# Masks of the first batch from 64-row tiles of TensorE, and block means of v from 32-column tiles

## The chip, the cores and the metric

One core of one Trainium2 chip runs the kernel; the other cores are idle. The metric is the device time of one execution in microseconds (us), from runs on the chip. A profiled execution also has a span: the time from its first to its last instruction.

## The reference, cut to what matters

Attention over 4 batches, 8 heads, 768 positions and 64 channels, in which a query sees the keys fewer than 16 positions away and, beside them, 24 block summaries (the maximum of each 32 keys, with the mean of the 32 values). Its output goes through a max-out layer.

```python
k_sum = k.reshape(B, H, nb, 32, D).max(axis=3)
v_sum = v.reshape(B, H, nb, 32, D).mean(axis=3)
mask_l = np.abs(pos[:, None] - pos[None, :]) < 16
scores_s = scale * einsum('bhsd,bhnd->bhsn', q, k_sum) + np.log(32)
scores_l = np.where(mask_l, scale * q @ k.T, -1e9)
a = softmax(concatenate([scores_l, scores_s]))
x = a @ concatenate([v, v_sum])        # to (3072 tokens, 512)
out = np.maximum(x @ w1, x @ w2) @ w_out
```

## The kernel before, in words

The max-out is rewritten: max(x w1, x w2) w_out is x (w1 w_out) + relu(x (w2 - w1)) w_out. So the kernel prepares wd = w2 - w1 (VectorE, line 662) and w1o = w1 w_out (TensorE, line 679), and each piece of 256 tokens needs "hidden" (x times wd, line 695, then a relu), and "out" (x times w1o, line 726, and the relu times w_out, line 733).

Attention is cut into batch, pair of heads (hp 0 to 3), and group (grp 0 to 2) of 256 queries. For each hp, "prep" casts k and q to bf16, turns them (on TensorE, line 471, or with a DMA transpose, line 475) and builds kx: for each of 12 tiles of 64 queries, 128 columns of keys, among them the 24 block maxima. "Scores" (line 540) multiplies 64 channels of one head with the tile's kx as the stationary operand and 64 queries as the moving one. The two heads of a pair (a = 0, 1) lie in partitions 0 to 63 and 64 to 127, so their products are matmuls on 64 of the 128 rows of the array, and they write two different PSUM banks. Then come exp on ScalarE over two pairs at once (line 558), "values" (line 594, the weights of a tile as stationary operand of 64 columns), a reciprocal (line 613), a product (line 616, "x"), and the turn of x (line 631 on TensorE in batch 0, line 622 by DMA transpose later).

The mask. `hide` holds 0 where a key is seen and -2^60 where not, as [128 keys, 64 queries] for an even and an odd tile (indices 0 and 1), and for the last two tiles (2 and 3, where 3 differs from 1). Batches 1 to 3 multiply the weights by a 0/1 mask on VectorE (line 566). Batch 0 adds `hide` on TensorE ahead of the scores: in each half task (one pair, one group; 12 of them) two matmuls (a = 0, 1), the identity stationary on all 128 rows, `hide` moving with 256 columns (line 531). TensorE thereby goes from 128-row to 64-row matmuls and back in each half task; the code calls this mode "NS" (N: whole array, S: 64 rows, V: column tiles).

The means of v. v is cast into vx with 32 positions in each 128-row chunk left over for a block mean. For batch 0 the means are kept apart (line 415, "apart"). For batches 1 to 3 `later_sums` adds up blocks with `amean`, whose columns mark the blocks: 6 chunks times two halves (u) of the head pairs, 12 matmuls on 64-column tiles with 256 moving columns (line 432). One copy ("means", 128x256) brings the sums into the staging tile `stg`, and four copies ("all sums", 32 partitions x 1584) put them into vx for both halves of the tile pairs w. On POOL only two of the four may run.

The order. Nothing is scheduled at run time. `Plan` gives each call of `op` a number in order of creation; ORDER lists the numbers in the order in which they are issued, HOMES gives each its engine (T TensorE, D VectorE, A ScalarE, P POOL, S the DMA queue of SP), SLOTS gives each buffer its place in its ring, and FILLS puts idle matmuls (line 189) ahead of some tasks. Each engine runs its list strictly in order. Loads (line 351), DMA transposes and most stores (line 744) share SP's queue. Loads go into 13 landing slots. Counting the calls of `op` turns the numbers into names; that is how the orders below were read.

Of the kernel before, what the change touches and what calls it, by code (L numbers as in the profile page):

```python
# [51 lines left out]
""".split()))  # L52
HOMES = "".join("""
    DPDPDDDPAAPPDDPDPPSSSPDDPTDDSSSDDPPTAASSSDDPPTDDSSSPDDATAASPTDSDTDSATASATDSASASDSASDSDSDSDTTATTATTDTTDDTATADPP
    ADPTDTADPPDDDTATADDDDDATPTDDDPPDTTATTDDTATTATTDDTDTTATTDDTATTATTDDTATTATTDDTDTTATTDDTASSSPSSSPSSSASSSDPDDPDDDD
    TADDDDDTDTDDAAPDDTPTDDDDAATADTDDSTADTDDSTADTDDSPTPTADAAAADTDTDDAPAATADTDDSTADTDDSTADTDDSSSSPSSSPSSSASSSADPPPPA
    APTDDAPAATATDDDPDDDTDTDDADAATADTDDSTADTDDSTADTDDSASDSADDPPASDSADPAPTADTDDSTADTDDSTADTDDSSSSPSSSASSSASSSDDPPPDP
    DPTADAAAASPSDDAAAPSDSADDADTADTDDSTADTDDSTADTDDSPSDSADDPDPSDSDDPPATADTDDSTADTDDSTADTDDSTTATTATTATTDTTTASTTTASTT
    DTTATTATTATTTASTTTDSTTATTATTATTDTTTDSTTTASTDTDTATATTTASTTTDSTATATDTATTTASTTTDSTDTATATDTTTASTTTASTATDTDTATTTDST
    TTASTATDTDTATTTASTTTDSTDTATATATTTASTTTDSTDTATATATTTASTTTASTATDTATDTTTASTTTASTATDTDTDTTTDSTTTASTTTDATTTAS  # L60
""".split())
SLOTS = list(map(int, """
# [12 lines left out]
""".split()))  # L75
FILLS = [
    (103, 9, 0), (113, 9, 0), (105, 1, 0)
]

class Ring:


# [62 lines left out]
def kernel(  # L147
# [276 lines left out]
    def later_sums(b, src, took):  # L424


        ps, st, cols = Buf(banks, "mm"), Buf(stg), H // 2 * D

        def sums():
            for m in range(NM):  # L430
# [401 lines left out]
```

## Time and profile before

| | us |
|---|---|
| median of 3 runs | 165.94 |
| lowest to highest | 165.39 to 166.05 |
| profiled execution, its own time | 166.49 |
| its span | 164.7 |

The profiled execution is 0.55 us above the median, and 1.79 us of its time lie outside the span. Its TensorE clock was granted in full throughout. In the rows below PE is TensorE's matmul, PEld its weight load, DVE VectorE, ACT ScalarE, SPq the queue of SP. A matmul's shown length holds its latency, so the cost of a series is read from starts and from the chain of work that ended last.

### The profile page before, as it was taken

To read this page: it belongs to the slowest core of one execution; us is meant where nothing else is said; L and a number is where in the kernel's file an instruction comes from. 1 tells how busy PE (TensorE), PEld (TensorE's weight loads), DVE (VectorE), ACT (ScalarE), POOL (GpSimd) and SP (SyncE) were. 2 spreads that over 40 slices of the span, in tenths; PEclk is the share of its full clock that TensorE was granted. 3 is DMA by queue.
4 is the path that set the end of the run, shared out by engine and by line. 5 is a ranking of instruction groups with operands and counts; after the bars stand their busy time and mean duration, and the time that the engine had idled before them with its cause. 6 is when DMAs were issued, how large, how long until landed. Compare 5 with 4: busy or idle time off the path is not lost.

```text
span 164.7 us, 4485 instructions
## 1 busy us (share of the span) xinstructions
PE 155.5 (94%) x1843; PEld 103.3 (63%) x1843; DVE 107.1 (65%) x214; ACT 100.7 (61%) x141; POOL 39.2 (24%) x73
## 2 busy tenths in 40 slices
PE   5699988999999999999799999999989999999993
PEld 2466677658886565477478555758645657885462
DVE  3568776887999599998288835995328684122110
ACT  6297798615677899895499571499854524142021
POOL 5265453022045001570441605604000000000000
PEclk9999999999999999999999999999999999999999
DMA  5999999999999999779999999699863334702133
GB/s 172 281 362 217 276 386 400 362 392 375 327 294 230 310 217 288 174 184 208 170 220 261 260 339 196 130 225 210 170 182 131 64 100 119 212 24 88 39 127 129
DMA packets 67188, 36.46 MB, mean 221 GB/s; under 512 B 54624, under 2 KB 61664, under 8 KB 67168
## 3 DMA queue, kind: packets, MB, share of 16 engines
q1 hardware_dynamic: 67024, 36.12, 88.3%
q8 instruction: 14, 0.23, 0.6%
q10 hardware_dynamic: 144, 0.07, 0.1%
q14 instruction: 6, 0.05, 0.1%
HBM read 25.17 MB, written 6.29 MB: 191 GB/s over the span
## 4 chain that ended last, share of the span: by engine, by line
PE 74%; DMA 10%; DVE 6%; ACT 3%; SPq 3%; issue 2%; DVEq 0%
PE banks L695 23%; PE banks L733 19%; PE banks L726 10%; PE banks L679 4%; PE banks L471 4%; DMA xt<-xs 3%; PE banks L594 3%; ACT pb L558 3%; DMA land<-in_q_dram 3%; PE banks L540 3%; DMA land<-in_k_dram 3%; PE banks L531 2%; SPq L622 1%; DMA out_dram<-o 1%; PE banks L189 1%
## 5 line engine op out<-in xcount | busy, mean ns | idle before, releaser
L733 PE MATMUL banks<-wo,g 128*128 128x512 bf16 (+2 forms) x208 | 47.3, 363 | 0.0
L695 PE MATMUL banks<-xt,wd 128*128 128x256 bf16 x384 | 46.2, 273 | 1.0 <-DMA xt<-xs 0.9
L695 PEld LDWEIGHTS <-wd 128*128 128x128 bf16 x384 | 37.5, 98 | 9.9 <-DMA xt<-xs 1.4
L733 PEld LDWEIGHTS <-g 128*128 128x128 bf16 x208 | 18.8, 98 | 16.7
L558 ACT ACTIVATE pb<-banks 128x1024 bf16<-128x1024 f32 x24 | 23.3, 1023 | 6.6 <-PE banks L540 6.5
L708 ACT ACTIVATE g<-banks 128x512 bf16<-128x512 f32 x29 | 16.8, 596 | 16.6 <-PE banks L695 16.6
L726 PE MATMUL banks<-w1o,xt 128*128 128x512 bf16 (+2 forms) x104 | 24.7, 363 | 0.0
L710 DVE TENSOR_SCALAR g<-banks 128x512 bf16<-128x512 f32 x19 | 12.9, 687 | 15.5 <-PE banks L695 15.5
L258 ACT COPY o<-banks 128x512 f32<-128x512 f32 (+2 forms) x17 | 9.5, 556 | 18.5 <-PE banks L733 15.1
L616 DVE TENSOR_TENSOR xs<-banks,inv 128x512 bf16<-128x512 f32 x24 | 16.1, 684 | 2.1 <-DMA xt<-xs 1.6
L497 DVE TENSOR_REDUCE ks<-kx 128x24 bf16<-128x768 bf16 x16 | 15.1, 946 | 1.5 <-ACT kx L258 1.3
L258 DVE COPY o<-banks 128x512 f32<-128x512 f32 (+1 forms) x9 | 5.8, 645 | 14.9 <-PE banks L733 10.7
L726 PEld LDWEIGHTS <-xt 128*128 128x128 bf16 x104 | 9.8, 98 | 8.8
L566 DVE TENSOR_TENSOR pb<-pb,mask 128x1024 bf16<-128x1024 bf16 (+1 forms) x24 | 13.3, 586 | 2.1 <-ACT pb L558 2.0
L258 POOL CAST kqb<-land 128x768 bf16<-128x768 f32 x9 | 8.8, 977 | 21.6 <-DMA land<-in_k_dram 17.3
L471 PE MATMUL banks<-ident,kqb 128*128 128x128 f32 x60 | 11.4, 311 | 2.0 <-DVE kqb L258 2.0
L258 POOL COPY vx<-vx 32x264 bf16<-32x264 bf16 (+4 forms) x15 | 11.7, 789 | 2.6 <-DMA land<-in_moe_w_dram 1.8
L594 PEld LDWEIGHTS <-pb 128*64 128x64 bf16 (+1 forms) x384 | 9.0, 110 | 4.3 <-issue 2.8
L258 POOL CAST vx<-land 128x768 bf16<-128x768 f32 x7 | 6.1, 877 | 22.3 <-DMA land<-in_v_dram 15.2
L258 DVE CAST kqb<-land 128x768 bf16<-128x768 f32 x15 | 9.0, 599 | 3.4 <-DMA land<-in_k_dram 2.0
L594 PE MATMUL banks<-vx,pb 128*64 128x65 bf16 (+1 forms) x384 | 10.7, 196 | 0.2
L471 PEld LDWEIGHTS banks<-ident,kqb 128*128 128x128 f32 x60 | 7.8, 158 | 4.9 <-DVE kqb L258 2.8
(84 smaller groups left out, 176.6 us busy)
## 6 DMA issues: line engine op xcount, KB each, us to landing
land<-in_k_dram SPq DMA_DIRECT2D x16, 384.0 KB, 5.8
land<-in_q_dram SPq DMA_DIRECT2D x16, 384.0 KB, 6.5
land<-in_v_dram SPq DMA_DIRECT2D x16, 384.0 KB, 6.2
out_dram<-o SPq DMA_DIRECT2D x19, 256.0 KB, 2.4
land<-in_moe_w_dram SPq DMA_DIRECT2D x8, 512.0 KB, 9.2
land<-in_moe_w_out_dram SPq DMA_DIRECT2D x4, 512.0 KB, 8.1
out_dram<-o SPq DMA_DIRECT2D x4, 224.0 KB, 2.5
xt<-xs SPq DMA_TRANSPOSE x18, 3.3
```

Of the source, the lines that this page charges most:

```text
L258: {"D": nc.vector.tensor_copy, "A": nc.scalar.copy, "P": nc.gpsimd.tensor_copy}[e](out=o, in_=i)
L471: nc.tensor.transpose(out=bank(ps)[:, 128 * j:128 * j + 128], in_=src.ap[:].bitcast(F32)[:, 128 * j:128 * j + 128], identity=ident32[:])
L497: op("D", 0.95, lambda e: nc.vector.tensor_reduce(out=ks.ap[:, 0:nb], in_=free(kt(), 128, [256, NM], [192, 2], [32, 2], [1, 32]), axis=AX. ...
L558: op("A", 1.03, lambda e: nc.scalar.activation(out=spread(pb.ap[:, 0, 0:1], [1, 1024]), in_=spread(bank_tile[:, ps.ap, 0:1], [1, 1024]), f ...
L566: on(e).tensor_tensor(out=o, in0=o, in1=spread(mask[:, 2 * u:2 * u + 1, 0:1], [0, n], [64, 2], [1, 64]), op=ALU.mult)
L594: nc.tensor.matmul(out=av(n)[64 * par:64 * par + 64, u, a, :], lhsT=pb.ap[r, at, 64 * par:64 * par + 64], rhs=vx[b].ap[r, par, hp + n, 2 * ...
L616: op("D", 0.69, lambda e: nc.vector.tensor_tensor(out=x.ap[:].rearrange("p n u a d -> p n (u a) d"), in0=spread(bank_tile[:, ps.ap, 0:1], ...
L695: nc.tensor.matmul(out=bank(ps)[:, 256 * s:256 * s + 256], lhsT=wd_tile[n // 2][:, c, at:at + 128], rhs=x.ap[:, c, :], start=(c == 0 and ( ...
L708: nc.scalar.activation(out=o, in_=bank(ps), func=ACT.Relu)
L710: nc.vector.tensor_scalar_max(out=o, in0=bank(ps), scalar1=0.0)
L726: nc.tensor.matmul(out=bank(ps, c1 - c0), lhsT=x.ap[:, c, sl], rhs=w1o[c].ap[:, cols], start=(c == 0), stop=False)
L733: nc.tensor.matmul(out=bank(ps, c1 - c0), lhsT=g.ap[:, f, sl], rhs=wo[f // 2].ap[:, f % 2, cols], start=False, stop=(f == FC - 1))
```

## The change: what it does, and its diff

The mask of batch 0: three of the four [128 keys, 64 queries] pieces of `hide` are turned once into `hidden_of` (queries on partitions, held twice, in 0 to 63 and 64 to 127), by six TensorE transposes into column tiles and a copy of 128x384. Each half task then adds the mask by matmuls on 64 rows: the turned mask stationary, 64 columns of the identity moving, twice over for two tiles (128 columns). Groups 0 and 1 have four of these, group 2 has six, as its last tile has another mask. The whole half task has mode "SS".

The later means of v: four 32-column tiles, one for each hp, with 128 moving columns, in place of two with 256: 24 matmuls in place of 12. The staging tile becomes 128x128. "All sums" becomes eight copies of 32x792 for four of 32x1584, each for one hp, and all may run on POOL.

```diff
+        turned = Buf(banks, "x")
+        def turn_hide():
+            for n, i in enumerate((0, 1, 3)):
+                for a in range(2):
+                    nc.tensor.transpose(out=bank(turned, 384, BF16)[64 * a:64 * a + 64, 128 * n:128 * n + 128],
+                                        in_=hide[:, i, :], identity=identity[:])
+        op("T", 0.23, lambda e: turn_hide(), words=12, mode="VV", read=[hide_in], write=[turned], label="turn hide")
+        copy("D", {"D": 0.34, "A": 0.5}, lambda: (
+            hidden_of[:].rearrange("p i k -> p (i k)"), bank(turned, 384, BF16)), read=[turned], write=[hidden_in],
+             port=False, label="hide turned")
...
-                for u in range(2):
-                    nc.tensor.matmul(out=bank(ps, cols)[64 * u:64 * u + 64], lhsT=amean[:, m, 0:64],
-                                     rhs=vx[b].ap[:, 0, 2 * u:2 * u + 2, m, :, 0:D], start=(m == 0), stop=(m == NM - 1))
+                for u in range(NP):
+                    nc.tensor.matmul(out=bank(ps, cols)[32 * u:32 * u + 32], lhsT=amean[:, m, 32:64],
+                                     rhs=vx[b].ap[:, 0, u:u + 1, m, :, 0:D], start=(m == 0), stop=(m == NM - 1),
+                                     tile_position=(0, 32 * u))
...
-                copy("D", {"D": 0.57, **({"P": 1.5} if u != w else {}), "A": 1.51}, aps,
+                copy("D", {"D": 0.32, "P": 0.79, "A": 0.85}, aps,
...
-                    for a in range(2):
-                        h = spread(hide[:, 0, 0:1], [0 if grp < NG - 1 else 128, 2], [1, 128])
-                        nc.tensor.matmul(out=bank(ps, second=a)[:, 256 * n:256 * n + 256].rearrange("p (i c) -> p i c", i=2),
-                                         lhsT=identity[:], rhs=h, start=True, stop=False)
+                    for at, i, count in ((0, 0, 2), (1, 1, 2)) if grp < NG - 1 else ((0, 0, 2), (1, 1, 1), (3, 2, 1)):
+                        for a in range(2):
+                            r = slice(64 * a, 64 * a + 64)
+                            nc.tensor.matmul(
+                                out=spread(bank(ps, second=a)[:, 256 * n + 64 * at:256 * n + 64 * at + 1],
+                                           [128, count], [1, 64]),
+                                lhsT=hidden_of[r, i, :], rhs=spread(identity[r, 64 * a:64 * a + 1], [0, count], [1, 64]),
+                                start=(at == 0), stop=False)
```

ORDER, HOMES, SLOTS and FILLS are new throughout (764 tasks before, 778 after). Where they matter here, by names (batch, hp, grp; a fourth digit is the pair of a half task; in "hidden" the digits are batch, grp, quarter; in "out" batch, grp, half):

```
TensorE, first scores, before:  turn k00 k02 k01 q00 q01 | scores 0010 0020 | turn k03 | 0000 0021 | turn q02 | 0011 | turn q03 |
                                0001 0200 0220 0201 | sums 06 04 | 0210 0221 0211 | values 0200 ...
TensorE, first scores, after:   turn k00 k02, turn hide, turn k01 q00 q01 | scores 0020 0010 | turn k03 | 0021 | turn q03 q02 |
                                0011 0000 0001 0200 0220 0210 0201 0221 | sums 06 04 | 0211 | values 0200 ...
TensorE, values 101/121 to the first hidden of (1, 1), before:  values 121 101, out x3, out 000, out 020, out 000, out 020, values 100 122,
                                sums 2, values 120, out 000, turn q20 | hidden 110
  after:                        values 121, out x2, turn q20, out x3, sums 2, values 122 100 120, out 000 | hidden 111
TensorE, sums of batch 1 to its first values, before:  sums 1, scores 120 100 101, out 001, turn k21, out 001, out 010, turn k20, scores 102 | values 121
  after:                        sums 1, out 001, scores 120 100 101, out 001, out 010, out 000, turn k20 | values 101
VectorE from x 101 to x 121, before:  x 101, weigh 120, weigh 100, wrap k20, inv 121, x 121
  after:                        x 101, cast v23, inv 121, x 121
SP's loads of the weights, before:  v00, w1 2, wo 0, w1 0, wo 1, w1 3, w1 1, wo 3, wo 2, w2 00, w2 01, k12, k13, w2 10, q12, w2 11
  after:                        v00, w1 2, w1 0, wo 1, wo 0, w1 3, w1 1, wo 2, wo 3, w2 00, k11, w2 01, k10, w2 10, k12, w2 11
"all sums" by engine:  before 6 VectorE, 5 ScalarE, 1 POOL; after 8, 9, 7
leftover pieces of v moved by DMA on SP's queue ("odd"):  before none, after 4
fillers:  before 9 ahead of turn k00, 9 ahead of turn k01, 1 ahead of turn q00; after 9, 3 (turn hide), 4 (turn k01), 3 (turn q01)
```

## Rows read from the trace of the kernel before

**Rows 1.** The page, chain that ended last: shares of the span by engine.

```profile
PE 74%; DMA 10%; DVE 6%; ACT 3%; SPq 3%; issue 2%; DVEq 0%
```

**Rows 2.** Stretches: length, busy PE, PEld, DVE, ACT, POOL (instructions), clock, DMA share, GB/s.

```profile
4.00:8.00 4.00, 2.31 (x10) 1.67 (x11) 2.47 (x7) 1.19 (x2) 0.72 (x5) 1.00 0.91 276
...
20.00:24.00 4.00, 3.75 (x126) 3.13 (x125) 3.15 (x9) 3.63 (x6) 2.19 (x4) 1.00 1.02 375
24.00:28.00 4.00, 3.19 (x116) 2.71 (x110) 2.33 (x7) 3.64 (x5) 1.57 (x3) 1.00 1.03 404
28.00:32.00 4.00, 4.00 (x46) 2.80 (x44) 3.48 (x9) 2.39 (x4) 0.00 (x0) 1.00 1.01 363
...
36.00:60.00 24.00, 24.00 (x259) 17.68 (x257) 20.03 (x34) 18.09 (x32) 5.86 (x8) 1.00 1.14 302
...
105.00:118.00 13.00, 13.00 (x94) 8.97 (x93) 9.05 (x17) 12.03 (x15) 2.58 (x5) 1.00 1.05 184
...
135.00:162.00 27.00, 26.90 (x196) 18.07 (x194) 6.74 (x12) 7.04 (x13) 0.00 (x0) 1.00 0.32 101
```

**Rows 3.** The chain in order of time: start, length, what.

```profile
16.21 0.33 PE banks L531 x2
16.54 0.22 PE banks L540 x8
...
28.77 0.86 PE banks L679 x4
...
31.84 4.41 PE banks L679 x20
...
55.90 0.60 PE banks L540 x36
...
68.32 1.20 SPq L622
...
101.48 0.89 PE banks L594 x48
```

**Rows 4.** Line 531, the mask: durations in ns, first and last start.

```profile
L531 PE MATMUL banks<-hide,identity x24: 270/273/283, 11.5 to 19.7; 128*128 128x256 bf16 x24
```

**Rows 5.** Timeline of PE, from 62 on: start, length, line, operation [idle before].

```profile
62.71 1.01 PE L594 MATMUL banks<-vx,pb 128*64 128x65 bf16 x32
...
70.34 0.82 PE L432 MATMUL banks<-vx,amean 128*64 128x256 bf16 x12
71.00 0.42 PE L594 MATMUL banks<-vx,pb 128*64 128x65 bf16 x16
...
72.55 1.04 PE L695 MATMUL banks<-xt,wd 128*128 128x256 bf16 x8
...
82.01 1.05 PE L695 MATMUL banks<-xt,wd 128*128 128x256 bf16 x8 [0.91 <-DMA xt<-xs]
```

**Rows 6.** Timeline of all engines, from 20.3 to 20.6.

```profile
20.47 0.12 PEld L599 LDWEIGHTS <-pb 128*64 128x64 bf16 x2
20.50 0.20 PE L599 MATMUL banks<-apart,pb 128*64 128x65 bf16 x2
20.50 0.12 PEld L594 LDWEIGHTS <-pb 128*64 128x64 bf16 x2
```

**Rows 7.** Timeline of ACT, from 12 to 66.

```profile
14.42 2.86 ACT L558 ACTIVATE pb<-banks 128x1024 bf16<-128x1024 f32 x3 [1.15 <-PE banks L540]
...
26.40 1.05 ACT L258 CAST wo<-land 128x1024 bf16<-128x1024 f32 x1
```

**Rows 8.** Timeline of DVE, from 20 to 60.

```profile
32.48 0.68 DVE L258 CAST wo<-land 128x1024 bf16<-128x1024 f32 x1
```

**Rows 9.** Timeline of PE, from 100 to 156.

```profile
121.56 0.55 PE L540 MATMUL banks<-kt,kx 64*128 64x64 bf16 x28 [0.39 <-DMA kt<-kqb]
```

**Rows 10.** Tile xt, the DMA transposes of x: from issue to landing.

```profile
DMA to landing us min/median/max: 2.4/3.3/5.8
```

**Rows 11.** Lines by shape: busy us, mean ns.

```profile
L258 POOL COPY vx<-vx 32x640 bf16<-32x640 bf16 x2 | 1.5, 774 | 0.0
```

More of the change, by code (lines that the diff above doesn't have):

```diff
@@ L24 @@
 ORDER = list(map(int, """
[27 rows of a table removed]
[27 rows of a table added]
 """.split()))
 HOMES = "".join("""
[L54 to L60, printed above, removed]
+    PDPDPDDDDAPPPDDTADPPSSSAAPPTAASSSDAPPTDASSSDDDDTADSSSPDDDTADSDTASDTDSPTASPTDSDSDSPSDSDSPSDSDTTDTTDTTATTADTDTAD
+    PAADPTATDDDPPDDTDTADDADDATDTADDPDDTTATTDDTATTATTDDTATTATTDDTATTATTDDTATTATTDDTATTATTDDTDSSSPSSSPSSSPSSSDDDDAPD
+    DSTDDDDDDDADATDTDDADADPTATDDDPPDTADTDDSTADTDDSTADTDDSPTPTDDPAADPTATADPAPDTADTDDSTADTDDSTADTDDSSSSPSSSASSSDSSSD
+    PAPAPPAATDPAPPAAADPTATADPAPAPTPTDDAPPDTADTDDSTADTDDSTADTDDSASPSDDAADPSPSDDPADTADTDDSTADTDDSTADTDDSSSSDSSSASSSD
+    SSSPPDSSDPPSTAAAAPPAPPPSDSDDPPAASASADADPTADTDDSTADTDDSTADTDDSPSASADAPAASPSDDADATADTDDSTADTDDSTADTDDSTTATTDTTDT
+    TATTTDSTTTASTTATTATTATTDTTTASTTTASTTATTATTATTATTTASTTTASTATATDTDTTTDSTTTASTATATDTATTTASTTTASTDTATATDTTTASTTTDS
+    TDTDTDTDTTTASTTTASTDTDTATDTTTDSTTTDSTATATATDTTTASTTTASTDTDTATDTTTASTTTDSTDTATDTATTTASTTTASTDTDTDTDTTTASTTTASTT
+    TDATTTAS
 """.split())
 SLOTS = list(map(int, """
[12 rows of a table removed]
[12 rows of a table added]
 """.split()))
 FILLS = [
-    (103, 9, 0), (113, 9, 0), (105, 1, 0)
+    (105, 9, 0), (15, 3, 1), (115, 4, 1), (117, 3, 1)
 ]
@@ L209 @@
     vxr = Ring(tiles("vx", 2, [128, 2, NP, NM, 2, VW], BF16))
-    stg = Ring(tiles("sums", 1, [128, H // 2, VW], BF16))
+    stg = Ring(tiles("sums", 1, [128, 2, VW], BF16))
     apart = tiles("apart", 2, [128, H, VW], BF16)
@@ L238 @@
     mask = const.tile([128, 4, 64], BF16, name="mask")
+    hidden_of = const.tile([128, 3, 128], BF16, name="hidden_of")
     amean = const.tile([128, NM, 128], BF16, name="amean")
@@ L242, in mark @@
         return Buf(Ring([None]))
-    hide_in, mask_in, amean_in, blocks_in, apart_zero, apart_in = (mark() for _ in range(6))
+    hide_in, hidden_in, mask_in, amean_in, blocks_in, apart_zero, apart_in = (mark() for _ in range(7))
     apart_of = [mark() for _ in range(NP)]
@@ L424, in later_sums @@
     def later_sums(b, src, took):
-        ps, st, cols = Buf(banks, "mm"), Buf(stg), H // 2 * D
+        ps, st, cols = Buf(banks, "mm"), Buf(stg), 2 * D
         def sums():
             for m in range(NM):
-                for u in range(2):
-                    nc.tensor.matmul(out=bank(ps, cols)[64 * u:64 * u + 64], lhsT=amean[:, m, 0:64],
-                                     rhs=vx[b].ap[:, 0, 2 * u:2 * u + 2, m, :, 0:D], start=(m == 0), stop=(m == NM - 1))
-        op("T", 0.68, lambda e: sums(), words=4 * NM, mode="VV", read=[*src, amean_in], write=[ps, *took],
+                for u in range(NP):
+                    nc.tensor.matmul(out=bank(ps, cols)[32 * u:32 * u + 32], lhsT=amean[:, m, 32:64],
+                                     rhs=vx[b].ap[:, 0, u:u + 1, m, :, 0:D], start=(m == 0), stop=(m == NM - 1),
+                                     tile_position=(0, 32 * u))
+        op("T", 0.42, lambda e: sums(), words=8 * NM, mode="VV", read=[*src, amean_in], write=[ps, *took],
            label=f"sums {b}")
-        copy("D", {"D": 0.41, "A": 0.37}, lambda: (
+        copy("D", {"D": 0.28, "A": 0.26}, lambda: (
             st.ap[:, :, 0:D], bank(ps, cols).rearrange("p (h d) -> p h d", d=D)),
              read=[ps, blocks_in], write=[st], port=False, label=f"means {b}")
-        for u in range(2):
+        for u in range(NP):
             for w, r in ((0, slice(96, 128)), (1, slice(32, 64))):
                 def aps(w=w, r=r, u=u):
-                    a = st.ap[32 + 64 * u:64 + 64 * u]
-                    return (vx[b].ap[r, w, 2 * u:2 * u + 2].rearrange("p g m a c -> p g m (a c)"),
-                            spread(a, [2 * VW, 2], [0, NM], [1, 2 * VW]))
-                copy("D", {"D": 0.57, **({"P": 1.5} if u != w else {}), "A": 1.51}, aps,
+                    return (vx[b].ap[r, w, u].rearrange("p m a c -> p m (a c)"),
+                            spread(st.ap[32 * u:32 * u + 32], [0, NM], [1, 2 * VW]))
+                copy("D", {"D": 0.32, "P": 0.79, "A": 0.85}, aps,
                      read=[st, *(took if w == 0 else [])],
-                     write=[vx[b], *(ready[b, hp] for hp in (2 * u, 2 * u + 1))], label=f"all sums {b}{u}{w}")
+                     write=[vx[b], ready[b, u]], label=f"all sums {b}{u // 2}{w}")
     def prep(b, hp):
@@ L546, in scores @@
             part = len(pairs) / 2
-            op("T", (0.25 + (0.53 if mask_on == "T" else 0) + (0.03 if grp == NG - 1 else 0)) * part,
+            op("T", (0.25 + (0.25 if mask_on == "T" else 0) + (0.03 if grp == NG - 1 else 0)) * part,
                lambda e, pairs=pairs: mm(pairs),
-               words=int((32 + (8 if grp == NG - 1 else 0)) * part) + (4 if mask_on == "T" else 0),
-               mode="NS" if mask_on == "T" else "SS",
-               read=[*(t[b, hp + n] for t in (kx, qx) for n in pairs), hide_in],
+               words=int((32 + (8 if grp == NG - 1 else 0)) * part) + ((8 if grp < NG - 1 else 12) if mask_on == "T" else 0),
+               mode="SS",
+               read=[*(t[b, hp + n] for t in (kx, qx) for n in pairs), *([hidden_in] if mask_on == "T" else [])],
                change=[ps], label=f"scores {tag}" + (str(pairs[0]) if mask_on == "T" else ""))
```

78 rows, old and new, of tables (ORDER, SLOTS) are left out of this document.

## The prediction, on record before the changed kernel ran

> **What bounds the kernel now.** I read the page's chain of waits first: the work that ended last is 74% TensorE [rows 1]. Then the stretches, where the reader should look at PE busy against the length, and at the DMA share beside it [rows 2]. From 36 to 60 PE is busy for all 24.00 us, from 135 to 162 for 26.90 of 27: there a cheaper matmul is time saved. From 20 to 28 it is busy 3.75 and 3.19 of 4 us while the DMA share is 1.02 and 1.03: the values of batch 0 and the weights are waited for, and a cheaper matmul may only give a longer wait. The chain in order of time joins the two: dense work begins with the first w1o at 28.77 [rows 3]. The sum of v lies in the dense part, the mask ahead of it, so the two savings are weighed apart.
>
> **The sums of v.** Before, 12 matmuls run from 70.34 to the next series at 71.00, with values on both sides: 0.66 us [rows 5]. A 512-column matmul takes 0.86 / 4 = 0.215 us [rows 3], so 128 columns take 54 ns and 256 take 107; 12 x 107 would be 1.29, so two column tiles already run together. After, 24 matmuls of 128 columns. Nothing here shows four column tiles at once. Bounds: all four together, 6 x 54 ns = 0.32; two at a time, 0.65; in turn, 24 x 54 ns = 1.3. The nearest row for a series of narrow matmuls in column tiles is values, 48 in 0.89 us or 18.5 ns each [rows 3]; 24 x 18.5 = 0.44. I take that: 0.22 saved three times, **0.66 us**, between +1.0 and a loss of 1.9. "All sums" has twice the copies of half the size. The nearest row on POOL, 32x640, took 0.774 [rows 11]. The new order puts four outs, scores and a turn between batch 1's sums and its first values, over 4 x 0.86 = 3.4 us [rows 3], and that covers them: nothing. Without this cover a late copy costs up to its 0.8 us.
>
> What stands in the way by a rule: the row shows weight loads beginning at 20.47 and 20.50 under matmuls in flight from 20.50, on the same 96 or 128 rows [rows 6]. The Trainium skill, "TensorE: Matmul & The Clock Gate", section "The mechanism", says that a weight load overlaps matmuls in flight only where the row group differs; the column tiles share all rows, so it would have them take turns. This case's trace does not agree with it for two column tiles; for four nothing here tells.
>
> **The mask.** The line's 24 matmuls start from 11.5 to 19.7 [rows 4], two in each of 12 half tasks. One takes 0.33 us and its eight scores 0.22 [rows 3], 0.55 together and 6.6 for all. The 0.22 holds the change of tile shape: in batch 1, 36 scores take 0.60, 16.7 ns each [rows 3], so eight are 0.13 and the change is 0.09. After, both parts have the same shape. Four mask matmuls of 128 columns take 2 x 54 ns = 0.11 if the two row tiles run together, 0.21 in turn; the scores of 16.7 ns, under the 27 ns that 64 columns need, show that row tiles overlap here, so I take 0.11. In the new order the half tasks stand in four runs, so four changes remain: 12 x (0.11 + 0.13) + 4 x 0.09 + 8 more matmuls of group 2 at 16.7 ns = 3.4 us. **3.2 us** less PE work, 2.0 if in turn.
>
> The turn of the mask is six transposes of 128 columns, at most 6 x 54 ns = 0.32. It lies near 8 us, where PE is busy 2.31 of 4 [rows 2] and in part with fillers, whose number is unchanged: nothing, or 0.3 if that idle time is gone. Its copy, 128x384, is well under the 1.05 us of ACT's 128x1024 [rows 7]; ACT idles 1.15 us for scores at 14.42 [rows 7], which covers it.
>
> How much of 3.2 arrives? The first exp waits for scores, so the first 1.15 us come through to ACT. The values then wait for v, whose loads do not move. First w1o starts at 28.77; its last input is cast by 26.40 + 1.05 = 27.45 [rows 3, 7]. So it can move up by 1.3 us at most with loads as they are. A second gate stands behind it: of the 20 matmuls from 31.84, the first eight need the early half of w_out, so those that need the last chunk start at 31.84 + 2 x 0.86 = 33.56, and its cast ends at 32.48 + 0.68 = 33.16 [rows 3, 8]. That leaves 0.4, unless the cast comes earlier; the new order gives that chunk to POOL, which does nothing from 28 to 32 [rows 2], though it is landing that counts. Between 0 and 1.3 I take **0.6 us**: over the second gate's 0.4, since its cast is taken out of a busy queue, and half of the first's bound.
>
> The loads keep their sequence nearly; one k load is moved ahead of a w2 chunk. Four leftover pieces of v go to SP's queue; each holds up the loads behind it for its issue, and the work is small beside a load: nothing, with PE's backlog as cover.
>
> **The sum.** 165.94 - 0.66 - 0.6 = **164.7**. The rows come from an execution of 166.49, 0.55 over the median; the differences are taken off the median.
>
> **Rivals.**
> *Loads set the pace.* The mask's saving only lengthens PE's waits before 28, and the sums' is lost ahead of the last batch. For it: DMA share 1.05 as late as 105 to 118 [rows 2], a wait of 0.39 for a DMA transpose ahead of batch 3's scores at 121.56 [rows 9], and 27 us of dense work behind them, with nothing left to fill a hole. Against it: those transposes sit in SP's queue behind those of x, which follow PE's work. 165.94 less 0 to 0.66: about 165.6. Chance 0.26.
>
> *More than I take.* The new order gets all of the 1.3 at the first w1o and loses the two waits of 0.91 and 0.39 [rows 5, 9]: 165.94 - 0.66 - 1.3 - 0.9 = 163.1, the smaller wait left in. For it: 3.2 us of PE work go. Against: the second gate. Chance 0.13.
>
> *Batch 1's x comes late.* Before, from the start of values 121 and 101 at 62.71, which take 0.9 or so, to the first hidden that needs their x at 72.55 is 8.9 us of other PE work [rows 5]. The second transpose is issued at 68.32 and lands by the median of 3.3 at 71.6, 8.0 us after the values [rows 3, 10]. In the new order only six outs, a turn, one sum and three values lie between: 6 x 0.86 + 0.33 + 0.44 + 3 x 0.3 = 6.8 us. With the chain as it was, PE would idle 1.2 us; with the longest landing, 5.8 for 3.3 [rows 10], 3.7: 164.7 + 3.7 = 168.4. It decides, on the slower side, from an idle time of 2.1 us. Against: VectorE has one cast between the two x in the new order, where it had two weighs, so the chain should be shorter. Chance 0.11.
>
> *The four column tiles take turns.* At 24 x 54 ns a sum costs 1.3 us, 0.64 more than now, three times: 165.94 - 0.6 + 1.9 = 167.2. Against: two tiles overlap now. By the rule of the Trainium skill cited above it would go this way. Chance 0.06.
>
> That leaves 0.44 for the forecast, whose own range is 163.9 to 165.2.
>
> **How the numbers follow.** 0.5%, about what a measurement of this kernel can tell from no change, is 0.83 us: faster is under 165.11, slower over 166.77. Faster: nearly all of the forecast and "more", 0.54. Same: loads and the forecast's edge, 0.29. Slower: x late, column tiles, 0.17. The range from 163.1 to 166.8 takes in "more" and the loads with one lost wait; it leaves out the slower two.
>
> **What would show it.** Right: the sums' series near 0.44 us with values beside it; mask and scores of a half task near 0.25, eight of the twelve changes of shape gone; first exp near 13.4; first w1o near 28; batch 3's scores and the last out each some 1.2 us earlier. Wrong: sums of 0.65 or more; half tasks near 0.35; the same start of w1o with a longer wait ahead; an idle stretch ahead of hidden 111, or one ahead of batch 3's scores that has grown by what was saved.

## The result, and the profile after

The changed kernel takes 168.21 us (median of 4 runs, 167.55 to 168.63) where the kernel before took 166.0 beside it (165.39 to 166.08): a ratio of **1.0138, 95% interval 1.0092 to 1.0184**. It is slower by 2.3 us, on the other side of the forecast and outside its range. Ratios here and below compare a kernel's faster executions alone, those within 1.5% of its fastest; the profiles of a_same, a_oddpool2, a_odd_fill and c_all (below) come from slower ones. The profiled execution of the changed kernel took 168.63, its span is 166.9 against 164.7 before.

The page: the engines' busy time, the row of granted clock in 40 slices of 4.2 us, one queue, and the chain's shares, which answer to [rows 1].

```profile
PE 155.3 (93%) x1917; PEld 104.3 (62%) x1917; DVE 111.9 (67%) x215; ACT 94.4 (57%) x141; POOL 51.2 (31%) x81
...
PEclk9999958799999999999999999999999999999999
...
q8 instruction: 15, 0.25, 0.7%
...
PE 76%; DMA 6%; ACT 6%; DVE 4%; issue 3%; POOL 3%; SPq 1%; POOLq 0%
```

The stretches of [rows 2], now of the changed kernel, with the columns given there:

```profile
20.00:24.00 4.00, 4.00 (x107) 3.53 (x101) 2.49 (x7) 3.52 (x6) 2.55 (x5) 0.62 1.03 370
24.00:28.00 4.00, 2.28 (x75) 1.86 (x75) 2.36 (x6) 1.95 (x4) 0.99 (x4) 0.93 1.04 405
28.00:32.00 4.00, 4.00 (x57) 2.67 (x52) 3.11 (x8) 1.01 (x1) 1.86 (x3) 0.60 1.05 382
36.00:60.00 24.00, 24.00 (x229) 17.72 (x228) 20.32 (x29) 14.38 (x25) 13.09 (x16) 1.00 1.06 280
...
135.00:162.00 27.00, 26.67 (x223) 17.57 (x223) 10.18 (x18) 4.02 (x7) 0.00 (x0) 1.00 0.25 69
```

The column after POOL is the granted clock. It was 1.00 in all these stretches before; now it is 0.62 from 20 to 24 and 0.60 from 28 to 32, half clock (1.2 of 2.4 GHz) for most of both. At these values TensorE's 12 us from 20 to 32 hold 4 x (0.38 + 0.07 + 0.40) = 3.4 us less clock than at the full level. The chain in order of time and TensorE's timeline show the parts of the change at work, and what came ahead of the falls:

```profile
7.30 0.59 PE banks L344 x6
...
14.44 2.87 ACT pb L576 x3
...
18.50 0.29 DVE apart L260
18.79 0.89 issue
...
25.25 1.72 issue
...
30.10 2.37 PE banks L697 x8
...
58.97 0.45 PE banks L446 x24
...
99.41 0.45 PE banks L446 x24
...
163.14 0.46 PE banks L751 x8
```

```profile
14.23 0.28 PE L546 MATMUL banks<-identity,hidden_of 64*128 64x128 bf16 x4
14.35 0.28 PE L558 MATMUL banks<-qx,kx 64*128 64x64 bf16 x8
14.46 0.28 PE L546 MATMUL banks<-identity,hidden_of 64*128 64x128 bf16 x4
...
17.55 0.22 PE L612 MATMUL banks<-vx,pb 96*64 96x65 bf16 x1
19.68 0.22 PE L612 MATMUL banks<-vx,pb 128*64 128x65 bf16 x1 [1.91 <-DVE apart L260]
...
25.06 0.19 PE L612 MATMUL banks<-vx,pb 96*64 96x65 bf16 x1
26.98 0.22 PE L612 MATMUL banks<-vx,pb 128*64 128x65 bf16 x1 [1.72 <-issue]
```

The first exp, in ScalarE's timeline:

```profile
13.03 1.03 ACT L576 ACTIVATE pb<-banks 128x1024 bf16<-128x1024 f32 x1
```

What to see. The parts themselves do what was forecast: the sums (line 446) take 0.45, and a half task's masks and scores 0.23, from 14.23 to the next at 14.46. The first exp starts at 13.03, 1.39 us ahead of the 14.42 of [rows 7], and the first values at 17.55; before they started at 20.12. But TensorE stops twice in the middle of a task, 1.91 and 1.72 us, between a first and a second matmul that read tiles of the same names. The first stop is put down to the cast of "apart", but that cast ended at 18.79; 0.89 us more pass with nothing the profile knows. After each stop the clock falls, and the first outer product of w1 and w_out comes at 30.10, partly at half clock (2.37 for eight), against 28.77 and 0.86 for four in [rows 3].

The balance of the span, by three stretches, first of after, then of before:

```profile
17.00:20.00 3.00, 1.09 (x38) 0.82 (x36) 1.96 (x7) 1.76 (x4) 0.00 (x0) 1.00 1.16 303
20.00:40.00 20.00, 18.28 (x291) 12.96 (x285) 14.74 (x26) 10.85 (x17) 8.73 (x12) 0.83 1.05 383
40.00:167.00 127.00, 122.11 (x1399) 80.72 (x1397) 81.85 (x149) 70.06 (x106) 35.62 (x44) 1.00 0.83 186
...
17.00:20.00 3.00, 3.00 (x64) 1.99 (x64) 2.16 (x7) 2.06 (x6) 1.26 (x2) 1.00 1.15 273
20.00:40.00 20.00, 18.94 (x328) 13.50 (x327) 15.31 (x31) 12.64 (x19) 6.00 (x9) 1.00 1.03 383
40.00:167.00 127.00, 120.36 (x1342) 79.18 (x1340) 78.98 (x150) 74.93 (x106) 23.50 (x32) 0.99 0.84 186
```

From 17 to 40 us TensorE idles 1.91 + 1.72 = 3.6 us after and 1.1 before, 2.6 more, and half clock takes the 3.4: 6.0 us lost where the masks were to save 3.2. That leaves 2.8, near the 2.4 that the last stretch tells.

At 40 us after has 122.11 us of TensorE's work left, before 120.36: 1.75 more, although its three sums are 0.2 cheaper each, so it has fallen 2.4 us behind by then. TensorE ends at 163.14 + 0.46 = 163.6 and, by the chain of before, at 161.9, so behind 40 us it idles 123.6 - 122.11 = 1.5 and 121.9 - 120.36 = 1.5. From TensorE's end to the span's end it is 3.3 and 2.8. That makes 1.75 + 0 + 0.5, the 2.2 between the spans. In this execution the loss is made before 40 us, but for 0.5 in the last output's copy and transfer. Behind 40 us the waits of 0.91 and 0.39 of [rows 5, 9] are gone, and three others stand in their place; the longest is of a new kind:

```profile
PE banks L612 <- DMA vx<-vx: 0.7, 1, 0.7
PE banks L713 <- DMA xt<-xs: 0.3, 1, 0.3
PE banks L558 <- POOL kx L260: 0.3, 1, 0.3
```

It is for a leftover piece of v. SP's queue shows why it is late:

```profile
121.74 0.64 SPq L258 DMA_DIRECT2D vx<-vx  x1
122.47 0.53 SPq L762 DMA_DIRECT2D out_dram<-o  x1
123.05 0.59 SPq L258 DMA_DIRECT2D vx<-vx  x1
123.73 2.42 SPq L762 DMA_DIRECT2D out_dram<-o  x2
126.21 0.59 SPq L258 DMA_DIRECT2D vx<-vx  x1
```

The third piece stands behind two outputs, one of which, by the profile, waits 1.2 us for ScalarE's exp; it is issued 3.2 us after the second and lands 2.23 us later, at 128.44 (the chain has both). The values of batch 3 start at 128.48.

### The profile page after: what moved, and what is told of

It is laid out like the page before. It is cut to its first block, busy times and chain, and to the rows that moved or that the text cites. A ratio compares the mean times of both kernels' runs of the same rounds, so it can differ in the third digit from the quotient of the medians.

```text
span 166.9 us, 4648 instructions
## 1 busy us (share of the span) xinstructions
PE 155.3 (93%) x1917; PEld 104.3 (62%) x1917; DVE 111.9 (67%) x215; ACT 94.4 (57%) x141; POOL 51.2 (31%) x81
## 4 chain that ended last, share of the span: by engine, by line
PE 76%; DMA 6%; ACT 6%; DVE 4%; issue 3%; POOL 3%; SPq 1%; POOLq 0%
PE banks L751 22%; PE banks L713 21%; PE banks L744 12%; PE banks L697 5%; PE banks L485 4%; PE banks L612 4%; PE banks L558 3%; DMA xt<-xs 3%; ACT pb L576 2%; DMA land<-in_k_dram 2%; POOL vx L260 2%; PE banks L668 1%; DMA vx<-vx 1%; PE banks L617 1%; PE banks L649 1%
## 5 line engine op out<-in xcount | busy, mean ns | idle before, releaser
L751 PE MATMUL banks<-wo,g 128*128 128x512 bf16 (+2 forms) x208 | 46.3, 363 | 0.0
L728 DVE TENSOR_SCALAR g<-banks 128x512 bf16<-128x512 f32 x25 | 17.0, 688 | 14.9 <-PE banks L713 14.7
L726 ACT ACTIVATE g<-banks 128x512 bf16<-128x512 f32 x23 | 13.3, 595 | 21.7 <-PE banks L713 21.5
L260 POOL CAST kqb<-land 128x768 bf16<-128x768 f32 x14 | 14.1, 1027 | 30.5 <-DMA land<-in_q_dram 11.3
L260 ACT COPY o<-banks 128x512 f32<-128x512 f32 (+2 forms) x19 | 10.5, 562 | 22.1 <-PE banks L751 21.1
L612 PE MATMUL banks<-vx,pb 128*64 128x65 bf16 (+1 forms) x384 | 11.8, 202 | 4.4 <-DVE apart L260 1.9
L260 ACT CAST kqb<-land 128x768 bf16<-128x768 f32 x11 | 10.4, 954 | 2.5 <-DMA land<-in_q_dram 1.6
L260 POOL COPY vx<-vx 32x640 bf16<-32x640 bf16 (+3 forms) x8 | 8.1, 1020 | 9.2 <-DVE vx L260 7.9
L260 DVE COPY o<-banks 128x512 f32<-128x512 f32 (+1 forms) x7 | 4.4, 629 | 9.4 <-PE banks L751 9.4
L558 PEld LDWEIGHTS <-kx 64*128 64x128 bf16 x416 | 7.6, 94 | 3.1 <-issue 2.1
```

The source lines that it names most:

```text
L260: {"D": nc.vector.tensor_copy, "A": nc.scalar.copy, "P": nc.gpsimd.tensor_copy}[e](out=o, in_=i)
L612: nc.tensor.matmul(out=av(n)[64 * par:64 * par + 64, u, a, :], lhsT=pb.ap[r, at, 64 * par:64 * par + 64], rhs=vx[b].ap[r, par, hp + n, 2 * ...
L726: nc.scalar.activation(out=o, in_=bank(ps), func=ACT.Relu)
L728: nc.vector.tensor_scalar_max(out=o, in0=bank(ps), scalar1=0.0)
L751: nc.tensor.matmul(out=bank(ps, c1 - c0), lhsT=g.ap[:, f, sl], rhs=wo[f // 2].ap[:, f % 2, cols], start=False, stop=(f == FC - 1))
```

## The experiments

Theory A: the early stage is paced by the arrival of TensorE's instructions, and the stops and the half clock behind them are the loss. Theory B: the new order is the slower one, by what it waits for. Five sets of runs follow, each on one chip beside the kernel before. All ratios are to the kernel before of the same set. "First product" is the first start of TensorE's outer products of w1 and w_out in that kernel's profile (28.6 before, 30.0 after).

### Each part alone, on the order of before

b_sums takes the new sums into the kernel before, b_masks the new masks with their turn, b_both the two; the order stays, but for one step that writes the mask, which goes from POOL to VectorE. b_pad38 adds as many matmuls as the masks do, and nothing else:

```
+    def pad(n):
+        for _ in range(n):
+            nc.tensor.matmul(out=bank_tile[0:32, 0, 0:2], lhsT=identity[:, 0:32], rhs=identity[:, 0:2], start=True,
+                             stop=True)
...
+            if t.label in ("turn k00", "turn k02"):
+                self.pad(19)
```

> The kernel before with its own plan; only the sums of v are new (24 matmuls of 128 columns, and each all-sums copy split in two on the engine that had it). Theory of the instruction stream (TensorE's instructions come in blocks of 16 KB, a block that comes late stops the engine early in the kernel, and the clock falls after the stop): the first 36 us stay as before, since the 36 added matmuls come after 57 us; three sums at 0.45 in place of 0.66, so 165.2 to 165.7 us. Rival, that the new plan's order alone is at fault: the same. If instead this is at or over 166.0, the sums' saving is lost ahead of the last batch.

> The kernel before with its own plan; only the mask of batch 0 is new (its turn and copy put right behind the last step that writes the mask, which goes from POOL to VectorE; sums of v as before). Theory of the instruction stream: TensorE comes to the end of its second block 2 to 3 us sooner and with 38 more matmuls behind it, and stops there, at its matmul 222 or within 10 of it, for 1 to 2 us, again near matmul 350 for over 1 us; the granted clock falls to half between 20 and 32 us in at least one stretch; first w1o at 29 to 30.5, time 166.2 to 168. Rival, that the new plan is at fault and the cheap mask is good: no such stop, first w1o at 27.5 to 28.5, time 164.7 to 165.6.

> The kernel before with its own plan and both parts of the change. Theory of the instruction stream: the time of the mask alone less 0.3 to 0.7, so 165.7 to 167.5, with stops near matmuls 222 and 350. Rival (new plan at fault): 164.0 to 165.2, no stops.

> The kernel before, unchanged in its work, plus 38 matmuls of 2 columns in TensorE's idle time ahead of the turns of k at 4 and 6 us, as many as the new mask adds. Theory of the instruction stream: the ends of blocks move up by 76 instructions against the work, so TensorE stops longer near its matmuls 222 and 350, counted with the added ones; first w1o 0.5 to 2 us later than 28.77, time 166.4 to 168. Rival, that only work and data count: the 38 take some 1 us of idle time, 165.8 to 166.3.

```
          ratio    95% interval       first product
b_sums    1.0114   1.0023 to 1.0205   29.0
b_masks   1.0151   1.0076 to 1.0226   28.8
b_both    1.0062   1.0014 to 1.0111   27.4
b_pad38   1.0137   1.0052 to 1.0223   28.7
```

None is faster, and the two parts together stand below each of them alone, so the ratios carry no more than their intervals. b_pad38, with no work saved or moved, stands as high as the changed kernel. Theory A's expectations were met in part only: b_masks stops for 0.50 and 0.89 us at other places than forecast, and its clock is at half from about 12 to 15 us, with no such stop ahead; b_both has no stop over 0.45 us and the earliest first product of these four, 27.4, and is not faster for it. b_sums shows what the sums give back without the new order. The lines are PE's timeline of b_sums, with the waits in brackets:

```profile
63.23 0.70 PE L591 MATMUL banks<-vx,pb 128*64 128x65 bf16 x25 [0.48 <-DVE kx L255]
64.52 0.29 PE L591 MATMUL banks<-vx,pb 128*64 128x65 bf16 x7 [0.59 <-DVE vx L255]
```

The values of batch 1 now wait 1.07 us for VectorE, where they did not before (in b_both the 0.48 came again, the 0.59 did not); the changed kernel, with its own order, has no such wait. b_pad38 shows stops like those of after, in two other tasks:

```profile
25.35 0.19 PE L601 MATMUL banks<-vx,pb 128*64 128x65 bf16 x1 [0.49 <-issue]
31.55 0.81 PE L686 MATMUL banks<-wo,w1t 128*128 128x512 bf16 x3 [0.89 <-issue]
```

### What the stops are

Numbering TensorE's instructions in order of start from 0 (weight loads, matmuls, and the four or five of its sequencer among them), and reading the transfers of the queue "instruction" from its DMA records (15 of 16 KB in after), gives the same picture in every kernel with such a stop. The columns: the instruction at which TensorE starts again, what it is, the end of the transfer ahead of it, its start, the difference in us.

```
kernel      instruction   what it is         transfer ends   starts    between
before          705       values                 25.19        26.60      1.41
after           449       values                 18.28        19.68      1.40
after           705       values                 25.45        26.97      1.52
after           961       transposes             32.03        33.44      1.41   (no stop)
b_pad38         705       values                 23.94        25.35      1.41
b_pad38         961       outer product          30.23        31.55      1.32
a_longfill      449       idle matmul            17.25        18.64      1.39
before          449       values                 18.36        21.03      2.67   (no stop)
```

The stops fall on instructions 449, 705 and 961, 256 apart, whatever the instruction is, and end 1.3 to 1.7 us after a transfer; in a_longfill (below) instruction 449 is an idle matmul that needs no data, and TensorE stops there all the same:

```profile
17.72 0.39 PE L197 MATMUL banks<-identity 128*128 128x512 bf16 x1
18.64 1.68 PE L197 MATMUL banks<-identity 128*128 128x512 bf16 x7 [0.53 <-issue]
```

The kernel before has such a stop too, at 705:

```profile
26.60 0.19 PE L599 MATMUL banks<-apart,pb 128*64 128x65 bf16 x1 [0.58 <-issue]
```

So TensorE waits for its own instructions. The transfers come no earlier in after than before (18.28 and 25.45 against 18.36 and 25.19), and the change brings TensorE to the end of a block sooner: at 17.8 and 25.25, where before it came to the first only at 21.0. It does so twice over: the masks take less time, and they and their turn are 38 matmuls more, each with its weight load, so that a block's end comes some 76 instructions earlier in the work. What sets the moment of a transfer was not tried. The Trainium skill, "Runtime: NRT & Kernel Launch", section "Instruction fetch mechanics", says that instructions are fetched in blocks of 256 and that a crossing is mostly hidden. The blocks agree with this trace; that they are hidden does not hold in this stage, where 1.9 and 1.7 us show.

### Taking single costs out of the changed kernel

a_merge adds the masks of both pairs with one matmul of 256 columns, 28 matmuls fewer. a_oldmask has the masks of before on the new order. a_longfill puts idle matmuls ahead of the two stopped tasks. a_oddpool gives the four leftover pieces of v from SP to POOL; the expectation speaks of POOL's queue, but what the edit does is that GpSimd copies them itself, without a DMA.

```
a_merge:     -  for n in pairs:  [128, count], [1, 64]
             +  if 0 in pairs:   [256 // per, 2 * per], [1, 64]
a_longfill:  +  if t.label in ("values 0200", "turn w1 2"):
             +      self.long_filler(6 if t.label == "values 0200" else 3)      # 8 matmuls of 512 columns
a_oddpool:   HOMES of the tasks "odd v" of batches 2 and 3:  SSSS -> PPPP
```

> The changed kernel, with the masks of both pairs of a group added by one matmul of 256 columns instead of two of 128: the same columns streamed, 28 fewer matmuls and so 56 fewer TensorE instructions (matmul and weight load) ahead of the values of batch 0. Theory A (the early stage is paced by the arrival of TensorE's instructions, in blocks of 256): up to 20 us the changed kernel's stops stand at its instructions 449 and 705, and the two resume 7.3 us apart; 56 of 256 instructions fewer are worth up to 1.6 us at the first outer product of w1 and w_out (30.1 there), the stops of 1.9 and 1.7 us shrink, and the time falls by 0.8 to 1.6 us, to a ratio of 1.004 to 1.009 to the kernel before. Theory B (the new order waits for data: loads of v, casts of w_out): the data come no earlier, first outer product at 30 again, ratio 1.014 as the changed kernel has. Theory C (only the fall of the granted clock counts): as B unless the clock stays up.

> The changed kernel's order and its new sums of v, with the masks added as before (identity stationary, one matmul of 256 columns in each row half and pair) and the turn of the mask left out. TensorE's mask work is back at 6.6 us from 3.4, so it comes to its instruction 449 some 3 us later, when its block has long landed. Theory A (instruction blocks): no stop over 0.6 us at 449 or 705, the granted clock stays full from about 11 us, first outer product at 28.5 to 29.5, ratio 0.997 to 1.006. Theory B (the new order itself is the slower one): 3.2 us more of work on the same order, nothing gained: ratio 1.014 or more, up to 1.03.

> The changed kernel with 8 idle matmuls of 512 columns (about 1.7 us, results unused) ahead of the two tasks nearest to its two stops, so that TensorE is busy where it stood. Theory A, in which the stops are waits for instructions: the stops shrink by about the filler's 1.7 us each, 16 matmuls (32 instructions) more lie ahead of the first outer product, and what is gained is the granted clock alone (0.98 in the profile of after, 3.4 us of work lost in it, about 1 us on average over its runs): ratio 1.005 to 1.014. If the stops were waits for data the same holds. Should the clock not matter, the ratio is 1.014 or above, by the 32 instructions up to 1.02.

> The changed kernel with the four odd pieces of v of batches 2 and 3 issued on POOL's queue instead of SP's. If their place on SP's queue (0.73 us of waiting at 128.5 us in the profile of after) is what the change loses, the time falls by up to 0.7 us, ratio 1.009 to 1.010; by theory A (the loss is made before 31 us) it stays at 1.012 to 1.016.

```
            ratio    95% interval       first product   stops at 449, 705
a_merge     1.0164   1.0086 to 1.0242   30.3            none, 0.79
a_oldmask   1.0105   1.0032 to 1.0179   29.7            none, 0.56
a_longfill  1.0042   0.9994 to 1.0089   29.1            0.53, none
a_oddpool   0.9997   0.9955 to 1.0039   28.6            1.67, none
```

Theory A foresaw two of these wrongly. With 56 instructions fewer (a_merge) the stops shrink and the time doesn't; with the old masks, 3.2 us more of TensorE's work, there is no large stop and full clock, and the first product is at 29.7 all the same. Both profiles have a wait of 1.1 us for a cast of w1 ahead of it, on which more below. Neither a_longfill nor a_oddpool can be read against the changed kernel here, which is not in this set; the next set has it. a_oddpool, which should have moved 0.7 us at most, stands lowest.

### The same edits beside the changed kernel

> The changed kernel itself, on the same chip as the three kernels beside it, so that the differences between the four are free of the chip. It is to stand at the ratio of the first comparison, 1.009 to 1.018; the other three are read against it.

> The changed kernel with the four odd pieces of v of batches 2 and 3 on POOL's queue, now beside the changed kernel. If the wait of 0.73 us at 128.5 us is all that they cost, 0.5 to 0.9 us below the changed kernel; if the step of 1.4 per cent that it showed against the kernel before holds on one chip, 2 us below; if that step was the chip's, no more than 0.3 us below.

> The changed kernel with 8 idle matmuls of 512 columns ahead of each of the two tasks nearest to its stops, beside the changed kernel. Theory A (the stops are waits for blocks of instructions, and what can be had back there is the granted clock): 0.7 to 1.7 us below the changed kernel, full clock from about 11 us in the profile. If the clock does not set the end: 0 to 0.4 us above it, by the 16 added matmuls.

> Both edits in one: odd pieces of v on POOL's queue and the idle matmuls. One lies before 31 us and one at 128 us, so their gains should add up: 1.2 to 2.6 us below the changed kernel, ratio to the kernel before 0.993 to 1.004. If both act on the same thing, no lower than the better of the two.

```
             ratio    95% interval       first product
a_same       1.0068   1.0026 to 1.0110   30.2
a_oddpool2   0.9931   0.9880 to 0.9982   29.3
a_longfill2  1.0056   1.0018 to 1.0094   29.8
a_odd_fill   1.0030   0.9993 to 1.0068   31.3
```

The changed kernel is slower here too, by less. Pieces copied by GpSimd are worth 1.4% without idle matmuls and 0.3% with them. The idle matmuls keep the clock up (0.997 and 1.000 in the profiles, 0.987 in a_same's) and are worth nothing that can be told: -0.1% in one pair, +1.0% in the other. In a_same's profile TensorE waits at three places from 14 to 34 us, and one of them is no block of instructions (a_merge, a_oldmask, c_few and a_oldodd have a wait of 1.06 us for this cast too):

```profile
PE banks L612 <- issue: 1.2, 1, 1.2
PE banks L612 <- DVE apart L260: 1.1, 1, 1.1
PE banks L668 <- POOL w1b L260: 1.1, 1, 1.1
```

POOL's timeline of a_same tells what the cast of w1 is behind:

```profile
20.43 0.95 POOL L260 COPY vx<-vx 32x640 bf16<-32x640 bf16 x2 [4.40 <-DVE vx L260]
22.42 0.71 POOL L260 COPY vx<-vx 32x640 bf16<-32x640 bf16 x1 [1.04 <-ACT vx L260]
23.19 0.14 POOL L401 MEMSET vx<- 32x48 bf16 x1
23.39 1.04 POOL L260 CAST w1b<-land 128x1024 bf16<-128x1024 f32 x1
```

POOL idles 4.40 us for VectorE, then copies pieces of v with another wait of 1.04 us between, and only then casts the chunk of w1 for which TensorE waits. In the kernel before ScalarE casts the first chunk of w1 at 22.42 and no such wait is there. In after's own profile the cast ends at 24.28, and TensorE, held up by its first stop, comes to it at 24.40.

### Fewer instructions, and the idle matmuls in float32

a_few takes a_merge's masks and turns the 19 early idle matmuls into five float32 ones of the same length, some 84 instructions fewer in all. a_fill32 has those five and float32 idle matmuls of 1.7 us at the two stops; c_few is a_few with the pieces on GpSimd; c_all has everything.

```
-        for _ in range(n): matmul(256 columns, bf16)
+        for c in range(0, 64 * n, 512): matmul(min(512, 64 * n - c) columns, float32)
```

> The changed kernel with the same masks in 28 fewer matmuls (one of 256 columns for both pairs) and the 19 early idle matmuls of 256 bf16 columns as 5 float32 ones of the same length: some 84 TensorE instructions fewer ahead of the first outer product, the same columns. Theory A (blocks of 256 instructions, 5.7 to 7.3 us apart where the engine waits for them): 84 of 256 are up to 2 us; the stops at instructions 449 and 705 fall under 0.8 us or vanish, the granted clock stays full once it has risen, first outer product 1.2 to 2 us ahead of the changed kernel's 30.0, ratio to the kernel before 0.998 to 1.006. Theory B (the loss lies in waits for data, the new order's): ratio 1.007 to 1.014 as the changed kernel's.

> The changed kernel with idle float32 matmuls of 1.7 us ahead of the two tasks nearest to its stops and the early idle matmuls as in the run beside it; all in all some 20 instructions fewer than the changed kernel. TensorE is busy where it stood, so that the granted clock should stay full: what it gains on the changed kernel is the clock's part. If the clock is worth 1 to 2 us of the 2.2 lost: ratio 1.000 to 1.006. If it is worth nothing: 1.007 to 1.014.

> The fewer instructions of the run beside it and the odd pieces of v on POOL's queue. Theory A and 0.7 us of the odd pieces: ratio 0.993 to 1.003, the lowest of the four if neither a clock fall nor loads stand in the way. Theory B: the odd pieces' 0.7 us alone, 1.003 to 1.010.

> All edits in one: fewer instructions, odd pieces of v on POOL's queue, and idle float32 matmuls of 1.1 us at the two places. If the fewer instructions have taken the stops away, the idle matmuls cost up to 2 us of TensorE's time in a stage that waits for loads anyway: 0 to 1 us above the kernel without them. If stops and clock falls are left, 0 to 1.5 us below it.

```
          ratio    95% interval       first product   stops at 449, 705
a_few     1.0117   1.0049 to 1.0184   29.1            0.53, 0.70
a_fill32  1.0101   1.0059 to 1.0143   29.2            none, none
c_few     1.0065   1.0018 to 1.0112   27.7            none, 1.05
c_all     1.0027   0.9976 to 1.0078   29.4            none, 0.62
```

Theory A falls as the one bound of the time. a_few and c_few, with 84 instructions fewer, stand 1.2 and 1.1 us at block ends where the changed kernel stood 3.6 and 2.2 (after and a_same), and their ratios, 1.0117 and 1.0065, are about those it had on other chips, 1.0138 and 1.0068. In a_fill32 there is no stop and full clock at 1.0101, but idle matmuls take the time there instead, so it tells of the clock alone. What takes the stops' place stands in the waits of a_few from 14 to 34 us:

```profile
PE banks L616 <- issue: 1.2, 2, 0.7
PE banks L696 <- DVE wo L261: 1.2, 1, 1.2
```

TensorE then waits 1.2 us for a cast of w_out. The pieces on GpSimd are worth 0.5% here (a_few to c_few), well inside the two intervals.

### The kernel before against itself, and the old masks without the odd pieces

> The kernel before, word for word, against itself: how far apart two sets of runs of one program come to stand. Expected: ratio 0.998 to 1.002; what it is off is to be taken off the ratios of the others, and its profile gives a second set of the early stage's times on another execution (first outer product, instructions 449 and 705, rise of the clock).

> The changed kernel's order with the masks of before (3.2 us more of TensorE's work ahead of 20 us, the turn of the mask left out) and with the four odd pieces of v copied by GpSimd as before instead of moved by SP's DMAs; the new sums stay. Theory D, in which the masks' saved work is worth nothing in this stage (loads and blocks of instructions take it back) and the odd pieces cost 0.5 to 0.9 us: ratio 0.995 to 1.004, as the changed kernel with the odd pieces on GpSimd had (0.9997 and 0.9931). If the masks' saving is worth the predicted 0.6 us or more, 1.003 to 1.012.

b_copy stands at 1.0007 (0.9952 to 1.0063): half a per cent is what one comparison can be off. a_oldodd stands at 1.0056 (1.0014 to 1.0098), first product at 30.3. Its expectation split the theories: 0.995 to 1.004 if the masks are worth nothing, 1.003 to 1.012 if they are worth the 0.6 us. It falls to the second, narrowly. With the new masks and the pieces on GpSimd the two comparisons gave 0.9997 and 0.9931. With the pieces on SP old masks stood at 1.0105 and new ones at 1.0138 and 1.0068, no gain. So the masks are worth 0 to 1.2%, on different chips; their size stays open.

## Why the prediction was wrong

**The sums, 0.66 us: right.** 24 matmuls take 0.45 (0.44 forecast). By the estimate of 54 ns for 128 columns they would take 1.3 in turn, so column tiles overlap here too. The cover held in the new order; b_sums, without that order, waited 1.07 us for VectorE behind the sums.

**The masks, 3.2 us less TensorE work: right.** A half task takes 0.23 us (forecast near 0.25), and line 546 last starts at 17.3 where line 531 last started at 19.7 [rows 4]. The turn alone was mis-sized: six transposes took 0.59 us, where 0.32 was to be the most.

**"Between 0 and 1.3 I take 0.6 us": this step failed.** Of the 3.2 us nothing arrived at the first product, which came 1.4 us later (28.6 to 30.0), and by 40 us TensorE was 2.4 us behind. The prediction bounded the share that arrives by the casts of w1 and w_out and by nothing else, below by nothing lost. First, it left out two limits between 17 and 30 us: the blocks of instructions, which the trace of before shows (0.58 us of "issue" at instruction 705), and what POOL does ahead of a cast of w1, which the new order brings. Once the masks were cheap, TensorE ran into the block end at 17.8 and stood 1.9 us, then 1.7. Second, a longer wait was taken to cost no more than what had been saved; here half clock followed, 3.4 us of clock in the profiled execution. On average that seems little: of the runs of a_same that count, the two with a clock under 0.99 took 168.4 us, the other seven 167.9. Nor does half clock follow every stop: after 1.18 us in a_longfill2 and 1.08 in b_copy the clock stayed full. In the experiments the limits stand in a row: blocks, w1's cast, w_out's cast; where one wait shrank, another of about 1 us showed. The first product lay between 27.7 and 31.3 in the kernels of the new order and between 27.4 and 29.4 in those on the order of before. How much of the loss each limit makes was not separated.

**"Four leftover pieces of v go to SP's queue ...: nothing, with PE's backlog as cover": this step failed too.** It looked at the loads behind the pieces, not at what stands ahead of them: outputs that wait for ScalarE. The cover was not there for batch 3, whose values wait 0.73 us. In three pairs on one chip each, GpSimd instead of SP's DMAs is worth 1.37, 0.26 and 0.52%, and 0.49% in a fourth over two chips; the mean is 0.66% or 1.1 us. Only the first pair's intervals lie apart, but all four have one sign. That this gain is the wait is argued, not shown: the wait itself ran from none (a_longfill2) to 1.39 us (a_oldmask), and in five of the six kernels with GpSimd's copies the sums of batch 3 wait 0.35 to 0.74 us for POOL instead.

**The tail was no term.** From TensorE's end to the span's end it is 0.5 us more.

**The rivals.** "Loads set the pace" came nearest: TensorE's waits before 28 us did grow, but for instructions first, not for loads alone, and it foresaw no loss. "Four column tiles take turns" is out (0.45), "x late" also: no wait stands ahead of hidden 111, and "more than I take" was not reached. Of the signs named, the half task, the sums and the first exp came (13.03, near 13.4 forecast); the exps that follow it start at 14.44, where the first one of before did, and the first product moved the wrong way.

**What stays open.** With the pieces on GpSimd the changed kernel stands at 0.993 to 1.000, close to the kernel before though 3.2 + 0.66 us of TensorE's work are gone; how much of what is missing the new order's early casts take, and how much the blocks, was not told apart. The new order cannot be all of it, since b_masks and b_both, on the order of before, are slower too; and as b_pad38 with its 38 idle matmuls is at 1.0137, it stays open whether any edit of this order costs about as much. No version was clearly ahead of the kernel before: a_oddpool's two comparisons do not agree on it.

## What to carry to other kernels

Before costing a saving in a stage that waits for loads, list every limit that lies within 2 us of the present one, the engine's own instruction blocks and the queue ahead of each cast included; the saving is worth at most the distance to the next of them. For a small transfer moved to a queue, look at what is ahead of it there and on what that waits, not at its own length. And count many short matmuls as instructions, too.

## What was not expected of the hardware

- TensorE stood for 0.5 to 1.9 us at instructions 449, 705 and 961, and went on 1.3 to 1.7 us after the transfer of a block had ended, an idle matmul among them.
- After two such stops, of 1.9 and 1.7 us, the granted clock was 0.62 and 0.60 in the stretches from 20 and 28 us; after stops of 1.1 to 1.2 us in b_copy and a_longfill2 it stayed full.
- Forecast, but on no row of four tiles: 24 matmuls of 128 columns on four column tiles took 0.45 us, 18.8 ns each, where one after the other they would take 1.3 by the estimate of 54 ns for one.
